# A down projection as seven block products, with weight sums made once and x in single loads

## The chip, the cores and the metric

The kernel runs on one core of a Trainium2 chip. The metric is the device time of one execution in microseconds (us). Times shown are medians over executions, and one further execution is recorded by the hardware profiler.

In the profile PE is TensorE (matmuls), PEld its weight loads, DVE is VectorE, ACT is ScalarE, POOL is GpSimd, and SP is the engine whose queue issues nearly all the transfers.

## The reference, cut to what matters

```python
x = A_x                                   # 1 x 2048 x 576
xn = layernorm(x)
q, k, v = split_heads(xn @ A_wqkv)        # 32 heads of 18
o = softmax(q @ k^T * 18**-0.5) @ v
s = merge_heads(o) @ A_wo
gate = xn @ B_W_gate                      # 576 -> 4608
up   = xn @ B_W_up
h    = relu(gate) * up                    # 2048 x 4608
g    = silu(h @ B_W_down)                 # 4608 -> 576: the down projection
return x + s * g
```

All is float32. The gated branch takes the normalized x, as the attention does.

## The kernel before, in words

**Precision.** Each float32 operand of a big product is split into a rounded high part and a low remainder ("hi" and "lo", type fp32r), and one product becomes three: hi x hi, hi x lo, lo x hi (`PRODUCTS`). ACT or POOL makes the high part with a copy, POOL or VectorE the low part with a subtraction.

**Row halves.** For the gated branch the 128 rows of TensorE are used as two halves of 64 (t = 0, 1), whose matmuls run side by side into different banks of PSUM. Where the halves change banks, a tiny ACT operation (`mark`) waits for the ends of both, and the next matmuls wait for it (`after`).

**Stages.** First come normalization, q, k and v. The parts of x for the gated branch, already split, are spilled to DRAM (`xTd`), by groups of 512 tokens (g = 0 to 3). Then 144 units follow, unit k standing for group g = k // 36 and one slice f = k % 36 of 128 hidden columns. Last comes the projection of the heads, 16 blocks of rows, with the gate applied.

**A unit** (`emit_unit`, L931). The 27 steps of `up(k)` make gate and up for 128 hidden columns and 512 tokens (9 chunks c of x, three products each). Between them an order written out by hand deals out the matmuls of the attention: from unit 16 on eight steps for scores and exponentials of one pair of heads (`exp_steps`) and eight for the row maxima of the next pair (`max_steps`, reduced by VectorE). Each row half serves one head, so a unit of 43 steps has 16 exponentials on ACT and 16 reductions. In the first 16 units there are no exponentials, and in the last eight no maxima. At the end `up_end` makes h = relu(gate) * up on ACT and VectorE, and `split_h` splits it into `hh`.

After an odd unit `attend` multiplies the exponentials with v. After an even unit `down(k - 1)` multiplies the last two units' `hh` with two slices of W_down (`rd`, split by POOL into `dw`): 4 blocks of 128 tokens x 2 halves of 288 output columns, each with 2 x 3 products and two row halves, 96 matmuls. Eight results of 128 x 288 are added to four sums `ys` (512 tokens x 576): VectorE adds six, and from unit 17 on the last two go through ACT (`add`) and POOL. Once a group is done, `gate_step` makes silu of the sums, one block of 128 tokens at a time, and stores it to `gd`.

**Queues and order.** TensorE, VectorE and POOL run in the order of the program (`mm`, `vec`, `gp` pin it). ACT's exponentials and relus, and from unit 17 on most of SP's transfers, are placed by a planner which simulates the machine; pinned ones keep their place behind what was traced before them. Buffers come from pools: five PSUM banks `psS` ("shared") rotate through scores, maxima and down products; two `psG` ("bank") hold gate and up; x has nine chunks (`xA`), read again for each group in the last unit of the group before, each as soon as its chunk is used for the last time (`load_x`, L295). `load_up` fetches the gate and up weights two units ahead; POOL splits them one unit ahead (`split_up`). Tile `e` has one buffer, shared by gates and additions.

Of the kernel before, what the change touches and what calls it, by code (L numbers as in the profile page):

```python
# [9 lines left out]
F32 = mybir.dt.float32  # L10
# [9 lines left out]
def kernel(  # L20
# [11 lines left out]
    P = 128  # L32
# [84 lines left out]
    xTd = dram.tile([NQ, XC, P, 2 * 512], F32, name="xTd")  # L117
    gd = dram.tile([S, D], F32, name="gd")
    od = dram.tile([D, S], F32, name="od")

    def bank(name):
        return psG.tile([P, 512], F32, tag="gen", name=name)
# [171 lines left out]

    def load_x(g, c):  # L295
        xc = xtile(xA)
        for t in range(2):
            pinned(
                nc.sync.dma_start(
                    xc[t * R : (t + 1) * R].rearrange("p a s -> p (a s)").bitcast(F32),  # L300
                    xTd[g, c // 2, c % 2 * R : c % 2 * R + R],
                )
            )
        xcur.setdefault(g, []).append(xc)

    with ExitStack() as st:
# [377 lines left out]
    wl = pool(mid, "wl", 2, "right")  # L684
    yp = pool(mid, "yp", 5, "right")

    def load_down(k):
        if k < len(units):
            f = units[k][1]
            if k == 1:  # L690
                rds[k] = hp.tile([P, 2, 512], F32, tag="hh", name="rd", bufs=3)
                rds[k] = rds[k].rearrange("p a s -> p (a s)")[:, :D]
            else:
                rds[k] = wl.tile([P, D], F32, name="rd", bufs=1)
            sp.dma_start(rds[k], wd[f * P : (f + 1) * P, :])

    def split_down(k):
        dws[k] = wl.tile([P, 2, D], F32R, name="dw")
        split_pool(dws[k][:, 0], dws[k][:, 1], rds.pop(k))

    def up(k):
# [27 lines left out]
    def up_end(k, ps):  # L729
        g, f = units[k]  # L730
        if f == NF - 1 and k + 1 < len(units):
            del xcur[g]
        h = hp.tile([P, 512], F32, name="h", bufs=1)
        ac.activation(h, ps[0], AF.Relu)
        vec(nc.vector.tensor_tensor(h, ps[1], h, ALU.mult))  # L735
        between.append((split_h, (k, h)))

    between = []
    hooks = {}
# [7 lines left out]

    ys = []

    def down(k):  # L750

        g, f = units[k]
        if f == 1:
            ys[:] = [yp.tile([P, D], F32, name="y") for _ in range(4)]
        terms = [(hhs.pop(k - 1), dws.pop(k - 1)), (hhs.pop(k), dws.pop(k))]
        steps = [(hh, w, a, b) for hh, w in terms for a, b in PRODUCTS]
        for q in range(2):
            parts = [(2 * q + m // 2, slice(m % 2 * HC, (m % 2 + 1) * HC)) for m in range(4)]
            outs_ = [(bank if m == 3 and q == 0 else shared)("py")[:, :HC] for m in range(4)]
            seen = []  # L760
            for turn_ in range(4):
                ends = []
                for i, (hh, w, a, b) in enumerate(steps):
                    for t in range(2):
                        rows = slice(t * R, (t + 1) * R)
                        m = ((0, 2, 1, 3), (1, 3, 0, 2))[t][turn_]
                        j, cs = parts[m]
                        ins = mm(
                            outs_[m], hh[rows, a, j * P : (j + 1) * P], w[rows, b, cs],
                            start=(turn_ < 2 and i == 0), stop=(turn_ >= 2 and i == len(steps) - 1),  # L770
                        )
                        if turn_ < 2 and i == len(steps) - 1:
                            ends.append(ins)
                        elif turn_ >= 2 and i == 0:
                            after(ins, seen[turn_ - 2])
                if turn_ < 2:
                    seen.append(pinned(nc.scalar.activation(mark, ident[:, :1], AF.Copy)))  # L777
                    for ins in ends:
                        after(seen[-1], ins)
                if q == 0 and turn_ == 1:  # L780
                    run_tasks(between)
                if q == 1 and turn_ == 3 and f > 1 and k > N1:
                    add = wl.tile([P, D], F32, tag="e", name="add", bufs=1)
                    for m in (2, 3):
                        ac.activation(add[:, parts[m][1]], outs_[m], AF.Copy)
                    gp.tensor_tensor(ys[3], add, ys[3], ALU.add)
                elif turn_ >= 2:
                    for m in range(2 * turn_ - 4, 2 * turn_ - 2):
                        j, cs = parts[m]
                        if f == 1:  # L790
                            nc.scalar.activation(ys[j][:, cs], outs_[m], AF.Copy)
                        else:
                            vec(nc.vector.tensor_tensor(ys[j][:, cs], outs_[m], ys[j][:, cs], ALU.add))  # L793
        if f == NF - 1:
            for j in range(4):
                gates.append((ys[j], g * 4 + j))
# [24 lines left out]
    def run_later():  # L821
        while later:
            later.pop(0)()
# [107 lines left out]
    def emit_unit(k, ex, ns, mx, nm):  # L931
        if k - 1 in rds:
            split_down(k - 1)
        if k not in rds and k not in dws:
            load_down(k)
        if k == 0:
            load_down(1)
        split_up(k + 1)
        if k and (units[k][1] < NF - 1 or k + 1 == len(units)):
            load_up(k + 2)  # L940
        if k == N1 + 1:
            sp.kept = False
        run_later()
        if k % 2:
            if k in rds:
                split_down(k)
            for _ in range(2):
                if to_load:
                    out_weights(to_load.pop(0))
        n = KC * len(PRODUCTS) + ns + nm  # L950
        ps, gens = up(k)
        order = []
        for t in range(2):
            due = []
            for cnt, gen, off, late in ((nm, mx, 0.0, LATE), (ns, ex, 0.25, -4)):
                due += [((i + off + t * 0.5) * (n - 1 + late) / cnt, gen[t]) for i in range(cnt)]
            due.sort(key=lambda d: d[0])
            ops = [gens[t]] * n
            free = n
            for when, gen in reversed(due):  # L960
                free = min(round(when), free - 1)
                ops[free] = gen
            order.append(ops)
        for i, (l, r) in enumerate(zip(*order)):
            next(l)
            next(r)
            if i == 8 or (i == 30 and k % 2 == 0):
                gate_step()
        if k == 0:
            split_up(2)  # L970
        up_end(k, ps)
        if k % 2 or k == 0:
            run_tasks(between)
        if k == 0:
            pinned(nc.scalar.activation(first_exp, ident[:, :1], AF.Exp))
        run_tasks(tasks)
        if k % 2:
            run_tasks(outs)
            while ready:
                attend()  # L980
        elif k:
            down(k - 1)


    wos = []

    def out_weights(c):
        rd = wl.tile([P, D], F32, name="rd", bufs=1)
# [77 lines left out]
    for u in range(NU):  # L1066
        ex = [exp_steps(u, h) for h in range(2)]
        more = u + 1 < NU
        mx = [max_steps(u + 1, h) for h in range(2)] if more else None
        if not more:  # L1070
            ac.kept = True
        for i in range(PER):
            if not more and i == 0:
                to_load[:] = range(4)
            if not more and i == PER - 1:
                fetch(0, gw_home())
                hooks[1] = [(out_weights, (4,))]
# [13 lines left out]
        split_heads(n)  # L1091
    run_tasks(outs)
    run_later()
    for n in range(16):
        if n == 2:
            down(len(units) - 1)
# [37 lines left out]
```

## Time and profile before

| | |
|---|---|
| median of 3 runs | 2584.05 us (2582.19 to 2586.38) |
| profiled execution | 2584.46 us, span 2582.7 us |
| instructions | 61529 |
| PE busy | 2569.2 us of the span |
| DVE busy | 1848.1 us |
| ACT busy | 1475.7 us |
| POOL busy | 1276.8 us |
| mean DMA rate | 99 GB/s |
| `down`, 72 times | 96 matmuls in some 6.5 us |

The page's part 5 and the answers by line give, for each group, the line, engine, operation, tile written and tiles read, then total busy time and mean of one in ns, then the idle time of the engine just ahead of it and what ended that. A line may be a helper's (L68 is every matmul, L85 every POOL operation), so groups are told apart by tiles. A timeline row gives start, duration in us (of merged instructions), engine, line, operation, tiles and count. [...]

### The profile page before, as it was taken

How to read it: one execution, taken by the hardware profiler on the slowest of the kernel's cores; microseconds unless marked ns; L12 is line 12 of the kernel's file. 1: busy time of each engine (PE TensorE's matmuls, PEld its weight loads, DVE VectorE, ACT ScalarE, POOL GpSimd, SP SyncE). 2: the span in 40 equal slices, each digit the busy share in tenths (PEclk: the TensorE clock that was granted, in tenths of full speed). 3: DMA queues.
4: the chain of work that ended last, by engine and by line, in shares of the span. 5: the costliest groups of instructions: out<-in, count | busy, mean ns of one | idle time of the engine just before them, and what ended most of it. 6: DMA issues, size and time to landing. Idle time of an engine off the chain costs nothing.

```text
span 2582.7 us, 61529 instructions
## 1 busy us (share of the span) xinstructions
PE 2569.2 (99%) x25301; PEld 2022.1 (78%) x25301; DVE 1848.1 (72%) x3019; ACT 1475.7 (57%) x3005; POOL 1276.8 (49%) x1003
## 2 busy tenths in 40 slices
PE   9999999999999999999999999999999999999999
PEld 8899987777677777877767777777777777777779
DVE  6336677777777778877777777887777777778127
ACT  3222146666666666666666666666656666666662
POOL 5246764444464444444455444444436444444555
PEclk9999999999999999999999999999999999999999
DMA  8866432323543223223263323332354233222237
GB/s 250 282 206 150 103 85 49 86 65 81 125 109 73 70 71 73 65 68 74 72 160 79 76 68 72 72 75 59 80 122 115 69 74 72 69 63 59 68 103 232
DMA packets 263833, 254.60 MB, mean 99 GB/s; under 512 B 27648, under 2 KB 208640, under 8 KB 263552
## 3 DMA queue, kind: packets, MB, share of 16 engines
q1 hardware_dynamic: 255808, 223.01, 35.1%
q0 software_dynamic: 7744, 27.66, 3.1%
q8 instruction: 199, 3.26, 0.5%
q14 instruction: 82, 0.67, 0.1%
HBM read 203.54 MB, written 46.53 MB: 97 GB/s over the span
## 4 chain that ended last, share of the span: by engine, by line
PE 95%; DMA 3%; POOL 1%; DVE 1%; ACT 0%; issue 0%; SPq 0%; POOLq 0%; ACTq 0%
PE pg L68 32%; PE py L68 18%; PE po L68 17%; PE pm L68 10%; PE psx L68 9%; PE pq L68 4%; PE pw L68 2%; DMA x<-xTd 2%; PE pv L68 2%; PE tps L76 0%; DMA rd<-in_A_wo_dram 0%; POOL gw L85 0%; DMA xt<-in_A_x_dram 0%; POOL y L85 0%; POOL kq L85 0%
## 5 line engine op out<-in xcount | busy, mean ns | idle before, releaser
L268 DVE TENSOR_REDUCE mx<-pm 128x1 f32<-128x512 f32 x2048 | 1371.6, 690 | 368.8 <-PE pm L68 261.9
L68 PE MATMUL pg<-x,gw 64*128 64x512 f32 x7533 | 1359.4, 392 | 6.0 <-DMA x<-xTd 6.0
L97 ACT ACTIVATE p<-psx 128x512 f32<-128x512 f32 x2048 | 1098.3, 604 | 208.6 <-PE psx L68 167.3
L68 PEld LDWEIGHTS pg<-x,gw 64*128 64x128 f32 x7533 | 1019.7, 186 | 106.4 <-DMA x<-xTd 10.2
L85 POOL TENSOR_TENSOR hh<-h,hh 128x512 fp32r<-128x512 f32 x144 | 185.7, 1289 | 808.2 <-ACT hh L743 804.5
L68 PE MATMUL py<-dw,hh 64*128 64x288 f32 x6912 | 478.2, 292 | 0.1
L68 PEld LDWEIGHTS py<-dw,hh 64*128 64x128 f32 x6912 | 473.3, 185 | 6.1 <-ACT h L97 0.7
L68 PE MATMUL po<-p,va 128*32 128x512 f32 x4096 | 452.7, 594 | 0.0
L85 POOL TENSOR_TENSOR gw<-rg,gw 128x1152 fp32r<-128x1152 f32 x131 | 350.2, 2673 | 10.5
L68 PEld LDWEIGHTS po<-p,va 128*32 128x32 f32 x4096 | 126.5, 110 | 291.5 <-issue 280.2
L793 DVE TENSOR_TENSOR y<-py,y 128x288 f32<-128x288 f32 x422 | 171.9, 453 | 140.0 <-PE py L68 140.0
L68 PE MATMUL psx<-qT,kq 56*128 56x512 f32 x608 | 230.8, 393 | 0.0
L68 PE MATMUL pm<-kq,qT 54*128 54x512 f32 x608 | 225.6, 395 | 0.3 <-ACT p L97 0.3
L85 POOL TENSOR_TENSOR dw<-rd,dw 128x576 fp32r<-128x576 f32 x144 | 206.5, 1434 | 11.5
L68 PE MATMUL psx<-kq,kA 56*128 56x512 f32 x512 | 195.2, 394 | 0.0
L68 PE MATMUL psx<-kq 56*128 56x512 f32 x512 | 194.8, 393 | 0.0
L68 PE MATMUL pm<-kA,kq 54*128 54x512 f32 x512 | 192.4, 398 | 0.5 <-ACT p L97 0.4
L68 PE MATMUL pm<-kq 54*128 54x512 f32 x512 | 191.1, 397 | 0.0
L85 POOL CAST gw<-rg 128x1152 fp32r<-128x1152 f32 x131 | 154.6, 1180 | 73.7 <-PE py L68 36.3
L777 ACT ACTIVATE mark<-ident 128x1 f32<-128x1 f32 x288 | 58.4, 203 | 219.1 <-PE py L68 219.0
L85 POOL TENSOR_TENSOR y<-add,y 128x576 f32<-128x576 f32 x61 | 87.4, 1433 | 180.0 <-ACT add L97 180.0
L743 ACT ACTIVATE hh<-h 128x512 fp32r<-128x512 f32 x144 | 90.8, 631 | 123.4 <-DVE h L735 123.4
(99 smaller groups left out, 2542.6 us busy)
## 6 DMA issues: line engine op xcount, KB each, us to landing
rd<-in_B_W_down_dram SPq DMA_DIRECT2D x144, 288.0 KB
rg<-in_B_W_gate_dram SPq DMA_DIRECT2D x131, 288.0 KB
rg<-in_B_W_up_dram SPq DMA_DIRECT2D x131, 288.0 KB
x<-xTd SPq DMA_DIRECT2D x72, 256.0 KB
qd<-hh POOLq DMA_DIRECT2D x16, 512.0 KB, 4.1
kd<-hh POOLq DMA_DIRECT2D x16, 512.0 KB, 5.6
xTd<-x SPq DMA_DIRECT2D x16, 512.0 KB
kq<-kd SPq DMA_DIRECT2D x210, 36.0 KB
```

Of the source, the lines that this page charges most:

```text
L68: return tc.keep_in_program_order(nc.tensor.matmul(*args, **kw))
L85: return lambda *args, **kw: tc.keep_in_program_order(op(*args, **kw))
L97: i = op(*args, **kw)
L268: vec(nc.vector.tensor_reduce(mx[:, h, b, j, c : c + 1], ps, axis=AX.X, op=ALU.max))
L743: copy = nc.scalar.activation(hhs[k][:, 0], h, AF.Copy)
L777: seen.append(pinned(nc.scalar.activation(mark, ident[:, :1], AF.Copy)))
L793: vec(nc.vector.tensor_tensor(ys[j][:, cs], outs_[m], ys[j][:, cs], ALU.add))
```

## The change

In groups 1 to 3 (54 of the 72 pairs of units) `down_made` takes the place of `down`. A pair's two slices of hidden columns, two halves of 256 tokens and two halves of 288 output columns make a 2 x 2 block product; by Strassen's identity seven products replace eight. Each product has 2 blocks of 128 tokens, three precision products and two row halves, opened in one visit of six matmuls and closed in a second, so a pair has 84 matmuls. The seven products are kept in seven sums a half group (`a`, `b`, `c`, `d`), added by ACT with POOL (seven of 14) and VectorE (seven); `combine` puts them together on POOL at the end of a group.

The left operands need sums and differences of blocks of h (`first_half`, `second_half`: POOL sums and lows, ACT high parts, emitted at steps 2, 8 and 13 of the following unit). The right ones need sums of blocks of W_down: `make_items` makes and splits all 18 x 7 of them during group 0, three in a unit up to unit 15 and five after that, and stores them to DRAM (`wtd`, 295 KB each); `load_w` reads seven a pair. The sums of weights are added on VectorE up to unit 15 and on POOL after it.

Also changed: a chunk of x is read by one transfer whose source is 64 rows taken twice, instead of two transfers; group 0's last `load_down` moves behind the steps of unit 35; `gate_step` moves from steps 8 and 30 to 17 and 27; `ys` has four buffers, not five; h has two.

```diff
     def load_x(g, c):
         xc = xtile(xA)
-        for t in range(2):
-            pinned(
-                nc.sync.dma_start(
-                    xc[t * R : (t + 1) * R].rearrange("p a s -> p (a s)").bitcast(F32),
-                    xTd[g, c // 2, c % 2 * R : c % 2 * R + R],
-                )
+        pinned(
+            nc.sync.dma_start(
+                xc.rearrange("p a s -> p (a s)").bitcast(F32),
+                xTd[g, c // 2, c % 2 * R : c % 2 * R + R].unsqueeze(0).to_broadcast([2, R, 1024]),
             )
+        )
...
+    MS = (0, 3, 4, 6, 2, 1, 5)
...
+    def first_half(h):
+        def raws():
+            nc.scalar.activation(a[:, 0, s], h[:, s], AF.Copy)
+            gp.tensor_tensor(r[:, s], h[:, z], h[:, s], ALU.subtract)
+            nc.scalar.activation(a[:, 0, z], r[:, s], AF.Copy)
+        def lows():
+            low(a, s, h[:, s])
+            low(a, z, r[:, s])
...
+        return {2: [raws], 8: [lows]}
...
+    def second_half(hs):
+        def raws():
+            nc.scalar.activation(b[:, 0, z], h2[:, z], AF.Copy)
+            gp.tensor_tensor(r[:, s], h2[:, s], h2[:, z], ALU.subtract)
+            nc.scalar.activation(b[:, 0, s], r[:, s], AF.Copy)
+            gp.tensor_tensor(r[:, z], h1[:, s], h2[:, z], ALU.add)
+            nc.scalar.activation(d[:, 0], r[:, z], AF.Copy)
+        def lows():
+            low(b, z, h2[:, z])
+            low(b, s, r[:, s])
+            low(d, s, r[:, z])
...
+            gp.tensor_tensor(r[:, :512], h1, h2, ALU.add)
+            nc.scalar.activation(c[:, 0], r[:, :512], AF.Copy)
+        def rest():
+            low(c, slice(0, 512), r[:, :512])
...
+        return {2: [raws], 8: [lows], 13: [rest]}
...
+    def down_made(k):
+        def visit(p, swap):
+            for i, (a, b) in enumerate(PRODUCTS):
+                for t in range(2):
+                    j = t ^ swap
+                    ins = mm(
+                        outs_[p][j], h[rows, a, (o + j) * P : (o + j + 1) * P], w[rows, MS[p], b],
...
+        def by_scalar(p, j):
+            src = add_home()
+            pinned(nc.scalar.activation(src, outs_[p][j], AF.Copy))
+            gp.tensor_tensor(dst, src, dst, ALU.add)
...
+        def opened(p):
+            outs_[p] = [(bank if j and p in (1, 4) else shared)("py")[:, :HC] for j in range(2)]
+            ends = visit(p, 0)
+            seen[p] = pinned(nc.scalar.activation(mark, ident[:, :1], AF.Copy))
...
+        def closed(p):
+            visit(p, 1)
+            by = (by_scalar, by_scalar) if p == 0 else (by_vector, by_vector) if p == 6 else (by_scalar, by_vector)
...
+        opened(0)
+        for p in range(7):
+            if p + 1 < 7:
+                opened(p + 1)
+            closed(p)
...
+        if f == NF - 1:
+            todo = [(combine, (j,)) for j in range(2)]
+                at_step[11] = [lambda: run_tasks(todo[:1])]
+                at_step[21] = [lambda: run_tasks(todo[1:])]
...
+    def make_items(fp):
+        def start(m, on):
+                    gp.tensor_tensor(t, x0, x1, op)
+            s_ = pw.tile([P, 2, HC], F32R, name="ws")
+            nc.scalar.activation(s_[:, 0], x0, AF.Copy)
+        def end(m):
+            gp.tensor_tensor(s_[:, 1], x0, s_[:, 0].bitcast(F32), ALU.subtract)
+            sp.dma_start(wtd[fp, m], s_.bitcast(F32))
...
-            if i == 8 or (i == 30 and k % 2 == 0):
+            if i in (17, 27):
                 gate_step()
+            if k < NF and k:
+                per = 3 if k < N1 else 5
+                if any(i == 2 + q * (n - 3) // per for q in range(per)):
+                    make_step(nc.vector if k < N1 else nc.gpsimd)
+            if k > NF:
+                pr = (k - 1) // 2
+                late = units[2 * pr + 1][1] == NF - 1 and 2 * pr + 2 < len(units)
+                if late == (k % 2 == 0) and i >= 1 and i % 4 == 1 and i // 4 < 7:
+                    load_w(pr % (NF // 2), [MS[i // 4]])
```

More of the change, by code (lines that the diff above doesn't have):

```diff
@@ L119 @@
     od = dram.tile([D, S], F32, name="od")
+    wtd = dram.tile([NF // 2, 7, P, 2, HC], F32, name="wtd")
     def bank(name):
@@ L683 @@
     pp = pool(mid, "pp", 8, "right")
-    wl = pool(mid, "wl", 2, "right")
-    yp = pool(mid, "yp", 5, "right")
+    wl = pool(mid, "wl", 1, "right")
+    yp = pool(mid, "yp", 4, "right")
+    plain = mid.enter_context(ExitStack())
+    pw = pool(plain, "pw", 2, "right")
+    made = mid.enter_context(ExitStack())
+    mw = []
     def load_down(k):
-        if k < len(units):
+        if k < NF:
             f = units[k][1]
@@ new lines, with load_w, sums_of @@
+    made_w = {}
+    def load_w(fp, ms):
+        if not made_w:
+            made_w["w"] = mw[0].tile([P, 7, 2, HC], F32R, name="w", bufs=1)
+        for m in ms:
+            sp.dma_start(made_w["w"][:, m].bitcast(F32), wtd[fp, m])
+    acc = {}
+    def sums_of(m, j):
+        a = acc["a", j], acc["b", j], acc["c", j]
+        return {
+            0: a[2][:, :HC], 1: a[1][:, :HC], 2: a[0][:, HC:], 3: a[2][:, HC:],
+            4: acc["d", 0][:, j * HC : (j + 1) * HC], 5: a[1][:, HC:], 6: a[0][:, :HC],
+        }[m]
@@ new lines, in combine @@
+    def combine(j):
+        a, b, c = acc["a", j], acc["b", j], acc["c", j]
+        l, r = slice(0, HC), slice(HC, D)
+        m5 = acc["d", 0][:, j * HC : (j + 1) * HC]
+        for d, s_, op in (
+            (a[:, l], c[:, l], ALU.add), (a[:, l], c[:, r], ALU.add), (a[:, l], m5, ALU.subtract),
+            (b[:, r], c[:, l], ALU.add), (b[:, r], b[:, l], ALU.subtract), (b[:, r], a[:, r], ALU.add),
+            (a[:, r], m5, ALU.add), (b[:, l], c[:, r], ALU.add),
+        ):
+            gp.tensor_tensor(d, d, s_, op)
@@ new lines, with load @@
+    items = []
+    def make_items(fp):
+        st = {}
+        def load():
+            st["w"] = pw.tile([P, 2, D], F32, name="wp", bufs=1)
+            for i in range(2):
+                f = 2 * fp + i
+                sp.dma_start(st["w"][:, i], wd[f * P : (f + 1) * P, :])
+        def start(m, on):
+            w = st["w"]
+            b = [[w[:, i, c * HC : (c + 1) * HC] for c in range(2)] for i in range(2)]
+            x0, x1, op = {
+                0: (b[0][0], b[1][1], ALU.add), 1: (b[0][0], None, None), 2: (b[0][1], b[1][1], ALU.subtract),
+                3: (b[1][0], b[0][0], ALU.subtract), 4: (b[1][1], None, None), 5: (b[0][0], b[0][1], ALU.add),
+                6: (b[1][0], b[1][1], ALU.add),
+            }[m]
+            if op is not None:
+                t = pw.tile([P, HC], F32, name="wt")
+                if on is nc.vector:
+                    vec(on.tensor_tensor(t, x0, x1, op))
+                else:
+                    gp.tensor_tensor(t, x0, x1, op)
+                x0 = t
+            s_ = pw.tile([P, 2, HC], F32R, name="ws")
+            nc.scalar.activation(s_[:, 0], x0, AF.Copy)
+            st[m] = x0, s_
+        def end(m):
+            x0, s_ = st.pop(m)
+            gp.tensor_tensor(s_[:, 1], x0, s_[:, 0].bitcast(F32), ALU.subtract)
+            sp.dma_start(wtd[fp, m], s_.bitcast(F32))
+        return [(load, start, end, m) for m in (None, 1, 4, 0, 2, 3, 5, 6)]
@@ L750, in down, with make_step @@
+    for fp in range(NF // 2):
+        items.extend(make_items(fp))
+    open_items = []
+    def make_step(on):
+        while open_items:
+            end, m = open_items.pop()
+            end(m)
+        if items:
+            load, start, end, m = items.pop(0)
+            if m is None:
+                load()
+            else:
+                start(m, on)
+                open_items.append((end, m))
     def down(k):
+        if k >= NF:
+            down_made(k)
+            return
         g, f = units[k]
@@ L933, in emit_unit @@
             split_down(k - 1)
-        if k not in rds and k not in dws:
+        steps = dict(at_step)
+        at_step.clear()
+        if k not in rds and k not in dws and k != NF - 1:
             load_down(k)
@@ L966, in emit_unit @@
             next(r)
-            if i == 8 or (i == 30 and k % 2 == 0):
+            for fn in steps.get(i, ()):
+                fn()
+            if i in (17, 27):
                 gate_step()
+            if k < NF and k:
[7 more added lines that the diff above has]
+                    load_w(pr % (NF // 2), [MS[i // 4]])
         if k == 0:
             split_up(2)
+        if k == NF - 1:
+            load_down(k)
         up_end(k, ps)
@@ L982, in emit_unit @@
             down(k - 1)
+            if k == NF:
+                while items or open_items:
+                    make_step(nc.gpsimd)
+                plain.close()
+                mw.append(pool(made, "mw", 1, "right"))
     wos = []
     def out_weights(c):
-        rd = wl.tile([P, D], F32, name="rd", bufs=1)
+        rd = wl.tile([P, D], F32, tag="e", name="rd", bufs=1)
         if c < 4:
@@ L1076 @@
                 fetch(0, gw_home())
-                hooks[1] = [(out_weights, (4,))]
+                hooks[5] = [(out_weights, (4,))]
                 hooks[2] = [(split_heads, (0,))]
@@ L1093 @@
     run_later()
+    for _, fns in sorted(at_step.items()):
+        for fn in fns:
+            fn()
     for n in range(16):
```

87 lines of the change are left out of this document (83 added, 4 removed).

## The prediction, on record before the run

> **What bounds the kernel now.** I read the page first: busy times and the chain that ended last.
>
> ```profile
> span 2582.7 us, 61529 instructions
> PE 2569.2 (99%) x25301; PEld 2022.1 (78%) x25301; DVE 1848.1 (72%) x3019; ACT 1475.7 (57%) x3005; POOL 1276.8 (49%) x1003
> PE 95%; DMA 3%; POOL 1%; DVE 1%; ACT 0%; issue 0%; SPq 0%; POOLq 0%; ACTq 0%
> ```
>
> TensorE is busy for 99% and carries 95% of the chain, so matmuls that go shorten the run, as long as what feeds TensorE keeps up. Then the groups of instructions by line; the durations below are the means of these rows.
>
> ```profile
> L68 PE MATMUL py<-dw,hh 64*128 64x288 f32 x6912 | 478.2, 292 | 0.1
> L793 DVE TENSOR_TENSOR y<-py,y 128x288 f32<-128x288 f32 x422 | 171.9, 453 | 140.0 <-PE py L68 140.0
> L97 ACT ACTIVATE add<-py 128x288 f32<-128x288 f32 x122 | 43.5, 409 | 80.0 <-PE py L68 80.0
> L777 ACT ACTIVATE mark<-ident 128x1 f32<-128x1 f32 x288 | 58.4, 203 | 219.1 <-PE py L68 219.0
> L85 POOL TENSOR_TENSOR gw<-rg,gw 128x1152 fp32r<-128x1152 f32 x131 | 350.2, 2673 | 10.5
> L85 POOL CAST gw<-rg 128x1152 fp32r<-128x1152 f32 x131 | 154.6, 1180 | 73.7 <-PE py L68 36.3 <-DMA rg<-in_B_W_up_dram 30.8 <-PE po L68 3.9
> L85 POOL TENSOR_TENSOR hh<-h,hh 128x512 fp32r<-128x512 f32 x144 | 185.7, 1289 | 808.2 <-ACT hh L743 804.5 <-DMA rg<-in_B_W_up_dram 2.5 <-DMA kq<-kd 1.1
> L85 POOL TENSOR_TENSOR y<-add,y 128x576 f32<-128x576 f32 x61 | 87.4, 1433 | 180.0 <-ACT add L97 180.0
> L85 POOL TENSOR_SCALAR e<-e 128x576 f32<-128x576 f32 x16 | 11.0, 686 | 0.1
> ```
>
> Last the windows and the timeline of one ordinary pair of units in group 2: 9.9 us of steps, 6.5 us of `down`, 10 us of steps, 7.1 us of `attend`.
>
> ```profile
> 1511.30:1521.20 9.90, 9.90 (x88) 8.50 (x86) 8.88 (x14) 9.23 (x17) 1.39 (x3) 1.00 0.32 68
> 1521.20:1527.70 6.50, 6.50 (x98) 6.46 (x96) 4.54 (x10) 2.04 (x6) 1.29 (x1) 1.00 0.12 27
> 1527.70:1537.70 10.00, 10.00 (x92) 8.85 (x88) 9.29 (x16) 9.22 (x18) 8.64 (x7) 1.00 0.12 31
> 1537.70:1544.80 7.10, 7.10 (x68) 1.98 (x64) 5.39 (x8) 1.23 (x2) 3.92 (x4) 1.00 0.72 167
> sum 33.50, PE 33.50 PEld 25.79 DVE 28.10 ACT 21.72 POOL 15.24; mean PE 8.38 PEld 6.45 DVE 7.03 ACT 5.43 POOL 3.81
> 1512.08 9.02 ACT L97 ACTIVATE p<-psx 128x512 f32<-128x512 f32 x16
> 1521.20 1.89 DVE L268 TENSOR_REDUCE mx<-pm 128x1 f32<-128x512 f32 x3
> ```
>
> Columns of a window: length, then busy time (and count) of PE, PEld, DVE, ACT, POOL, clock, DMA share, GB/s. TensorE never pauses in the pair, at full clock. ACT's sixteen exponentials fill the steps, and VectorE is still reducing 1.9 us into `down`.
>
> **The products.** `down` issues 96 matmuls a pair, `down_made` 7 x 2 x 6 = 84. A matmul costs 478.2 us / 6912 = 69 ns, two row halves running together. Twelve fewer in 54 pairs: 54 x 12 x 69 ns = **-44.8 us**. That is all the change can take from the matmuls.
>
> **Banks and evacuations in the product.** Evacuations of 288 columns rise from 8 to 14 a pair (7 on ACT, 7 on VectorE): 7 x 409 + 7 x 203 ns of marks = 4.3 us on ACT in a 5.8 us product, so ACT has room; what matters is when. A visit of six matmuls takes 0.41 us. The third product opens after three visits, 1.2 us in, and needs the fourth and fifth shared bank; VectorE's last reduction (to 1523.1) frees the fifth only 1.7 us or so after `down` began: 0.4 us of waiting, where the old order needed that bank 3.3 us in. The first mark comes after one visit instead of two (0.1 us), and the fourth product needs both banks that ACT alone evacuates. ACT's copies further on wait for a home in `e`, which is free when POOL has added (about 0.8 us each, below). I take 0.65 us a pair, **+35 us**; bounds 0.1 and 1.0 us (no waiting but the first mark; each of these waits in full), +5 to +54. So the products alone are nearly a draw.
>
> **Splitting the hidden sums.** The new 256-column operations cost POOL about 0.7 us and 288 columns 0.8 us (from 1289 ns at 512 and 1433 ns at 576, 2.2 ns a column). POOL loses the splits of `dw`, gains 8 such pieces, two of 512 and seven adds, and stays near 22 us of a 33.5 us pair: hidden. ACT gets copies of 256 and one of 512 columns among exponentials that fill 9.0 of 9.9 us; half a microsecond of lateness is bridged by the five banks. I take 0.15 us a pair, **+8 us** (0 to +25).
>
> **Weight sums in group 0.** 126 products are made in units 1 to 35, with 37 MB stored by SP. From unit 16 a pair holds ten items, some nine with a product: 9 x 0.8 us of subtractions and 6 x 0.8 us of adds on POOL, on top of its 15.2 us, 27 us; between add and subtraction it waits for ACT's copy (some 0.6 us, 6 times), 31 us of 33.5. POOL is then almost the bound, ACT queues behind it, and each copy needs a `ws` buffer whose store has landed. 1.5 us in ten pairs: **+15 us** (0 to +40). SP's stores stand ahead of loads that are issued a unit before use: no cost while that unit covers them.
>
> **x in single loads.** This carries the forecast. Now the boundary of a group:
>
> ```profile
> 1291.81 0.36 SPq L97 DMA_DIRECT2D rd<-in_B_W_down_dram  x1
> 1292.27 16.12 SPq L299 DMA_DIRECT2D x<-xTd  x18
> 1309.10 0.65 SPq L97 DMA_DIRECT2D rg<-in_B_W_gate_dram  x1
> 1294.00:1308.00 14.00, 14.00 (x126) 7.53 (x124) 8.59 (x15) 7.37 (x15) 4.97 (x4) 1.00 1.03 237
> 1304.40:1317.80 13.40, 11.33 (x93) 8.47 (x91) 9.11 (x14) 9.73 (x18) 0.00 (x0) 1.00 1.08 225
> 1317.56 1.72 PE L68 MATMUL py<-dw,hh 64*128 64x288 f32 x21
> ```
>
> Eighteen loads of 256 KB saturate all 16 DMA engines at 237 GB/s; the unit takes 13.4 us of which 2.1 are idle, and its `down` starts at 1317.6. The new load halves SP's issues, and no `rd` load stands ahead of it. But its source is a pattern of 2 x 64 rows, the outer 2 with no stride. How many engines does a load get? Compare one load of `nr` (outermost dimension 2) with one `rd` load (128 rows), each alone in its window:
>
> ```profile
> DMA  0000000000000111110000000000000000000000
> DMA packets 18, 0.00 MB, mean 3 GB/s; under 512 B 18, under 2 KB 18, under 8 KB 18
> DMA  0018999359016393898959698661302010000000
> DMA packets 144, 0.29 MB, mean 147 GB/s; under 512 B 16, under 2 KB 16, under 8 KB 144
> q1 hardware_dynamic: 144, 0.29, 51.9%
> ```
>
> `rd` has 128 rows and 16 small packets more, and its slices reach 9 tenths of the engines; `nr` has 16 runs and 2 small packets more, and never passes 1 tenth, as 2 of 16 engines would (0.125). So I read: a load is spread by its outermost dimension, and a source whose outermost dimension is 2 runs on two engines. Each then moves 256 KB a load. Speed of a busy engine: 237 GB/s / (16 x 1.03) = 14.4 GB/s at saturation, 0.29 MB / (0.519 x 16 x 2 us) = 17.5 for `rd`, and from the row of the other queue,
>
> ```profile
> q0 software_dynamic: 7744, 27.66, 3.1%
> ```
>
> 27.66 MB / (0.031 x 16 x 2582.7 us) = 21.6. With two engines alone I take the fastest: 262144 B / 21.6 = 12.1 us a load, 109 us for nine (18.2 and 164 us at saturation; 80 us if a lone engine is a third faster than any row). From 1288.5, when the first buffer is free, the last x lands near 1399 and `down` could start at 1400 instead of 1317.6: **+82 us**, at the three boundaries **+247 us** (160 to 410).
>
> [...]
>
> **Behind the loads.** `rg` shares those two engines and lands after x; POOL's in-order queue has `split_up(73)` (1.2 + 2.7 us) ahead of `second_half`, so the hidden sums come some 9 to 11 us after x, at two boundaries. In the next unit `combine` puts 16 x 0.8 us and the four gates 4 x (0.7 + 1.4) us on POOL, beside two `gw` splits of 3.9 and some 9 of hidden sums: 38 us for a 33.5 us pair, before POOL's own waits for the gates' Tanh: the following `down_made` waits about 10 us and its `b` sums, still being stored by the gate, 3 more. Together 2 x 24 = **+48 us** (10 to 60). At the start the seven x loads issued by 116 us, and the last two at 196 us, are late too:
>
> ```profile
> 82.01 33.72 SPq L299 DMA_DIRECT2D x<-xTd  x14
> 195.88 4.10 SPq L299 DMA_DIRECT2D x<-xTd  x3
> L68 PE MATMUL pg<-x,gw x7533: 383/392/502, 199.3 to 2505.1; 64*128 64x512 f32 x199
> ```
>
> Two loads at 12.1 us from 196 end near 222, where unit 0 would want the last x some 7 us after its start at 199: **+20 us** (0 to 45). The weight loads (2 MB a pair) run a unit ahead: 0.
>
> Sum: -45 + 35 + 8 + 15 + 247 + 48 + 20 = +328 on the profiled execution's 2584.46 us (span 2582.7; the median, 2584.05, is the same within 0.02%): **2912 us**. With all bounds low 2715, high 3174; they will not all go one way: 2760 to 3080.
>
> **Rivals.** (1) *All sixteen engines.* If the load is spread by the 128 rows of its destination, x costs no more than now, and 2 to 3 us a boundary go because no `rd` load delays SP: -8. If POOL's chains are hidden as well (their low ends), the sum is -45 + 20 (downs) + 4 + 5 - 8 = -24: **2560 us, faster**. It decides at SP's loads in units 35, 71 and 107: under some 26 us for nine loads they hide in their two units. For it: the destination does have 128 rows, and the old loads with 64 ran at 237 GB/s. Against it: `nr`, whose source has 16 partitions, still ran on two. (2) *All sixteen engines, but POOL and ACT eat the gain:* -45 + 35 + 8 + 15 + 48 - 8 = +53 - some slack: **2630 us**. For it: VectorE's 1.9 us tail and POOL's 38 us. (3) *Draw:* the waits in the product equal its twelve matmuls and the loads are hidden: **2585 us**.
>
> **Chances.** The two-engine load 0.68; rival 1 0.17; rival 2 0.11; rival 3 0.04. Within 0.2% (5 us) is what a measurement here can't tell from no change. Faster 0.17, same 0.04, slower 0.79. To leave out no more than 2 in 10 the range goes from 2570 to 3060; the likeliest case's own is 2760 to 3080.
>
> **What would show it.** Right: small packets fall by 36 x 30 for x (two a load instead of 2 x 16); in units 36, 72 and 108 DMA share near 0.13 for 80 to 160 us, with TensorE idle and released by x<-xTd; matmuls py down by 648; POOL busy near nine tenths in units 16 to 35; a TensorE wait for hidden sums after each x. Wrong: x at the old bandwidth, or steps at boundaries of 10 to 14 us; then the forecast is too high by some 300 us. If `down_made` lasts under 5.9 us, my bank waits are not there.

## The result

| | before | after |
|---|---|---|
| median | 2583.12 us (2582.09 to 2586.38, 4 runs) | 3605.05 us (3602.46 to 3614.0, 4 runs) |
| ratio | | 1.3959, 95% interval 1.3932 to 1.3987 |
| profiled execution, span | 2584.46, 2582.7 us | 3614.0, 3612.2 us |
| mean granted clock of TensorE | 1.000 | 0.876 |

Slower, as forecast, but by 1022 us and not by 328. The page of the kernel after: span, the row of busy times, the granted clock in 40 slices (tenths of full speed), and the chain that ended last.

```profile
span 3612.2 us, 63126 instructions
PE 2920.0 (81%) x24653; PEld 2138.8 (59%) x24653; DVE 1898.3 (53%) x3118; ACT 1710.9 (47%) x3761; POOL 1737.2 (48%) x1762
PEclk9978888888868989998976999899985999999899
PE 31%; POOL 31%; DMA 9%; ACT 5%; issue 4%; SPq 1%; DVE 0%; ACTq 0%; POOLq 0%; DVEq 0%
```

TensorE has 648 matmuls fewer and is busy for 351 us more, since its clock fell from 1.000 to 0.876. The chain, 95% TensorE before, now runs as much over POOL, though POOL is busy for only 48%. The waits of TensorE, ACT and POOL (engine and tile, what released it; us in total, times, longest):

```profile
PE psx L68 <- ACT p L97: 422.5, 135, 42.4
PE pg L68 <- DMA x<-xTd: 72.7, 12, 10.1
ACT ha L779 <- POOL hr L85: 233.8, 54, 13.3
ACT hb L802 <- POOL hr L85: 211.0, 54, 45.7
ACT ws L965 <- DMA wtd<-ws: 168.6, 42, 19.0
ACT hc L817 <- POOL hr L85: 163.2, 54, 3.0
POOL gw L85 <- PE pg L68: 436.7, 46, 10.4
```

TensorE waits for a bank that ACT's exponentials (`p`) have not emptied; ACT waits for POOL's sums of the hidden values (`hr`, 54 times each, once a pair) and for the weight sums (`ws`); POOL in its turn waits for TensorE to free the weights' buffer (`gw`). In an ordinary pair of group 2, timeline and windows (here and below, rows in between are left out):

```profile
2631.72 3.09 POOL L85 TENSOR_TENSOR c<-add,c 128x288 f32<-128x288 f32 x4 [11.79 <-ACT add L879]
2634.76 2.33 POOL L85 TENSOR_TENSOR y<-add,y 128x288 f32<-128x288 f32 x3
2637.04 1.14 POOL L85 CAST gw<-rg 128x1152 fp32r<-128x1152 f32 x1
2638.26 2.63 POOL L85 TENSOR_TENSOR gw<-rg,gw 128x1152 fp32r<-128x1152 f32 x1
2640.84 0.73 POOL L85 TENSOR_TENSOR hr<-h 128x256 f32<-128x256 f32 x1
...
2641.60 0.42 ACT L779 ACTIVATE ha<-hr 128x256 fp32r<-128x256 f32 x1 [4.23 <-POOL hr L85]
2641.92 2.06 ACT L97 ACTIVATE p<-psx 128x512 f32<-128x512 f32 x4
...
2642.55 0.79 PE L68 MATMUL psx<-qT,kA 56*128 56x512 f32 x1 [3.46 <-ACT p L97]
2643.64 0.63 PE L68 MATMUL psx<-qT,kA 56*128 56x512 f32 x1
2648.68 0.39 PE L68 MATMUL psx<-qT,kA 56*128 56x512 f32 x1
```

```profile
2636.30:2653.10 16.80, 13.34 (x90) 9.90 (x92) 9.94 (x16) 9.35 (x18) 6.74 (x8) 0.80 0.56 159
1150.00:1825.00 675.00, 605.41 (x5103) 423.75 (x5105) 431.89 (x702) 400.13 (x870) 334.58 (x345) 0.91 0.33 93
```

ACT's copy of `hr` is in its queue ahead of the exponentials. POOL reaches `hr` only after its seven additions of the product before (5.4 us) and the split of the next weights (3.8 us), so ACT stands 4.23 us, TensorE 3.46 us, and behind the pause a matmul takes some 0.62 instead of 0.39 us for over 5 us. The steps of this unit last 16.8 us; POOL was busy for 6.7 of them. A pair (from one product's start to the next) takes 42.4 us in group 1, where before took 33.7. Over 1150 to 1825, 15.9 such pairs, TensorE stood 69.6 us, 4.4 a pair: half of the 8.7 lost. Most of the rest is the clock of 0.91: 0.09 x 675 us are 61 us, 3.8 a pair, less what fell into the pauses themselves.

The following runs take the changed kernel apart. For e1 to e4 the time is that of one execution (before: 2584.16 us beside them), for the others a median, with the ratio to before and its interval.

### The profile page after: what moved, and what is told of

It is laid out like the page before. It is cut to its first block, busy times and chain, and to the rows that moved or that the text cites. A ratio compares the mean times of both kernels' runs of the same rounds, so it can differ in the third digit from the quotient of the medians.

```text
span 3612.2 us, 63126 instructions
## 1 busy us (share of the span) xinstructions
PE 2920.0 (81%) x24653; PEld 2138.8 (59%) x24653; DVE 1898.3 (53%) x3118; ACT 1710.9 (47%) x3761; POOL 1737.2 (48%) x1762
## 4 chain that ended last, share of the span: by engine, by line
PE 31%; POOL 31%; DMA 9%; ACT 5%; issue 4%; SPq 1%; DVE 0%; ACTq 0%; POOLq 0%; DVEq 0%
PE pg L68 15%; POOL gw L85 12%; PE psx L68 6%; PE pm L68 5%; POOL hr L85 5%; POOL y L85 4%; POOL c L85 4%; DMA x<-xTd 3%; PE py L68 3%; ACT p L97 2%; DMA rg<-in_B_W_up_dram 2%; POOL hb L85 2%; PE pw L68 1%; SPq L97 1%; DMA wtd<-ws 1%
## 5 line engine op out<-in xcount | busy, mean ns | idle before, releaser
L68 PE MATMUL pg<-x,gw 64*128 64x512 f32 x7533 | 1624.8, 439 | 86.4 <-DMA x<-xTd 72.7
L68 PEld LDWEIGHTS pg<-x,gw 64*128 64x128 f32 x7533 | 1135.5, 212 | 238.3 <-DMA x<-xTd 79.3
L85 POOL TENSOR_TENSOR c<-add,c 128x288 f32<-128x288 f32 x204 | 157.9, 807 | 584.3 <-ACT add L879 584.3
L68 PE MATMUL psx<-qT,kA 56*128 56x512 f32 x416 | 185.8, 461 | 119.3 <-ACT p L97 119.3
L68 PE MATMUL pm<-kA,kq 54*128 54x512 f32 x512 | 220.2, 455 | 28.8 <-DMA kA<-kd 19.0
L68 PEld LDWEIGHTS psx<-qT,kq 56*128 56x128 f32 x608 | 128.4, 211 | 161.4 <-ACT p L97 146.2
L68 PE MATMUL pm<-kA,qT 54*128 54x512 f32 x416 | 172.1, 436 | 23.9 <-ACT p L97 23.9
L739 DVE TENSOR_TENSOR h<-pg,h 128x512 f32<-128x512 f32 x144 | 98.3, 683 | 159.5 <-ACT h L97 107.6
L965 ACT ACTIVATE ws<-wt 128x288 fp32r<-128x288 f32 x90 | 39.8, 443 | 298.6 <-DMA wtd<-ws 158.5
L68 PEld LDWEIGHTS psx<-kq 56*128 56x128 f32 x512 | 110.9, 217 | 114.7 <-ACT p L97 101.8
L68 PEld LDWEIGHTS psx<-kq,kA 56*128 56x128 f32 x512 | 109.0, 213 | 116.8 <-ACT p L97 104.1
```

Of the source, the lines that this page charges most:

```text
L68: return tc.keep_in_program_order(nc.tensor.matmul(*args, **kw))
L85: return lambda *args, **kw: tc.keep_in_program_order(op(*args, **kw))
L965: nc.scalar.activation(s_[:, 0], x0, AF.Copy)
```

## Experiments: where the 1022 us lie

**e1, x in two loads again.** The changed kernel with the old `load_x`.

```diff
-            nc.sync.dma_start(xc..., xTd[g, c // 2, ...].unsqueeze(0).to_broadcast([2, R, 1024]))
+        for t in range(2):
+            nc.sync.dma_start(xc[t * R : (t + 1) * R]..., xTd[g, c // 2, ...])
```

> The changed kernel with x loaded as before, in two transfers of 64 rows a chunk. Theory A (the single load runs on two of 16 engines, and this is one of three separate losses): the units at the three group boundaries fall from 82 to some 13 to 16 us and the start loses its 30 us, so about 240 us come off 3605: 3340 to 3400 us. Rival (x only hides other waits, which then show): under 100 us come off.

3367.39 us: the single load costs 238 us here.

**e2, the kernel before with the single load of x alone.** The opposite edit on the other kernel.

> The kernel before with nothing changed but the single load of x. Theory A: nine loads of some 10 us on two engines, +60 to 75 us at each of three boundaries and +20 to 35 us at the start: 2790 to 2850 us. Rival (in the changed kernel the loads were slow because the weight loads queued with them): within 30 us of 2583.

2865.14 us, +281. In its trace the boundary pairs take 113.0 us instead of 36.3 to 37.0 (76 each; forecast 82). The start costs 50 us, where 20 were forecast and 45 was the bound: unit 0 starts at 228.8 instead of 199.3 us, and its first product at 270.3 instead of 220.2. SP's queue and TensorE's waits from 190 to 300 us:

```profile
81.66 74.88 SPq L298 DMA_DIRECT2D x<-xTd  x7
PE pm L68 <- DMA kA<-kd: 19.0, 1, 19.0
PE po L68 <- DMA x<-xTd: 17.1, 2, 10.3
```

The first seven loads hold SP's queue for 74.9 us instead of 33.7, so loads of the attention behind them (`kA`) come late too, and inside unit 0 TensorE waits for the last two chunks of x. These waits are 36 of the 50 us. Page and window of e2, busy share of the DMA engines in 40 slices of 1432 to 1502 us:

```profile
DMA packets 262752, 254.59 MB, mean 89 GB/s; under 512 B 26568, under 2 KB 207560, under 8 KB 262472
DMA  1111111111111111161111111111111111111111
GB/s 51 56 51 51 51 48 41 51 54 51 54 51 51 51 51 51 68 166 44 51 54 51 54 51 35 49 54 51 51 51 54 51 51 51 51 51 51 54 51 51
```

Small packets (under 512 B) fall from 27648 to 26568, by 1080 = 36 x 30, two a load instead of 32; the share is one tenth and the rate 51 GB/s, some 25.5 for each of two engines. A load takes some 10.2 us (I had 12.1 from 21.6 GB/s).

**e8, the same single loads from 128 plain rows.** This kernel reads another chunk's rows in half of the places.

```diff
-            xTd[g, c // 2, c % 2 * R : c % 2 * R + R].unsqueeze(0).to_broadcast([2, R, 1024])
+            xTd[g, min(c // 2, 3)]
```

> The kernel before with x in single loads whose source is 128 plain rows in place of 2 x 64 with no stride between (half of the rows read are another chunk's, so the values are not x's; bytes, destination and number of loads are those of the change). Theory (the outermost dimension of the source sets the engines: 2 gave 2): 16 engines, no loss at the change of group, 2575 to 2588 us, 52 to 53 x-free packets fewer a group and DMA share near 1 there. Rival (any single load of this size is slow, or the destination or SP's order is at fault): 2800 us or more, as with the pattern of 2 x 64.

2576.71 us, ratio 0.9975 (0.9966 to 0.9984): 7 us under before, about what rival 1 gave x on sixteen engines (-8). The window 1288 to 1308 us:

```profile
DMA  0079999579648988998899999999999999999999
q1 hardware_dynamic: 2654, 5.64, 92.1%
```

Same bytes, same destination, as many loads, and all engines work: the pattern of the source was the cause. Its 2 in the outermost dimension came with a stride of zero, and no run here takes only one of them away; the prediction's `nr` loads, with a 2 and no such stride, never passed 1 tenth either, which speaks for the 2.

**e3, the hidden sums ahead of the splits.** e1 with POOL's split of the next weights moved behind the first sums, and ACT's copies of the results some steps later, so that they find them ready.

```diff
-        return {2: [raws], 8: [lows]}
+        return {2: [raws], 9: [high], 10: [lows]}     # high: ACT's copy of hr
...
-        split_up(k + 1)
+        steps.setdefault(10 if k % 2 else 14, []).append(next_up)     # split_up and load_up
```

> x in two loads, and from unit 37 on POOL does the hidden sums before the split of the next gate and up weights (which moves from the start of a unit to step 10 or 14), with ACT's copies of the late sums placed where the sums are ready. No work is added or taken away. Theory B (ACT, in order, stood waiting for POOL's sums behind that split, and TensorE behind ACT): an ordinary pair of units in groups 1 to 3 falls from some 42.5 us to 34 to 36, some 300 to 450 us less than with x alone: 2920 to 3080 us. Rival C (ACT's additional copies themselves, or the 2 MB of weight loads a pair, slow the steps): less than 80 us under x alone.

2999.64 us: with the same instructions 368 us are gone. Ordinary pairs take 34.4 us. Over 12.7 of them TensorE is busy without a break at full clock:

```profile
1150.00:1586.00 436.00, 435.95 (x4033) 315.10 (x4031) 333.86 (x557) 313.68 (x685) 270.62 (x274) 1.00 0.40 111
```

**e4 and e5, one pair's weight sums alone.** e1 (e4) and e3 (e5) with the sums of the first pair of slices only, read by all pairs; 17 of 18 pairs are left out.

```diff
-    for fp in range(NF // 2):
-        items.extend(make_items(fp))
+    items.extend(make_items(0))
```

> x in two loads, and the weight sums of the first pair alone are made; every pair reads these seven. It leaves out 17 of 18 pairs of weight sums with their loads, copies and stores. Theory D (the sums in group 0 cost some 290 us by holding ACT): units 0 to 35 fall to some 10 us over those of before, 250 to 300 us under x alone: 3070 to 3130 us. Rival (what holds group 0 is the slow start after x): under 80 us.

> Three repairs at once: x in two loads, POOL making the hidden sums ahead of the next weights' split, and only the first pair's weight sums (17 of 18 pairs of slices are left out, so the numbers it multiplies with are not the reference's). If the three losses are independent, as my theory says, the rest adds: e3's 2999.6 minus the 261.5 us that e4 took off e1 = 2738 us (2715 to 2765), and what is left over before (154 us) lies in the pair after each change of group (some 30 us each, combine and the gates on POOL), in the last pairs and in some 0.7 us an ordinary pair. Rival: the losses overlap (one slow engine hidden behind another), then 2650 us or less, or over 2800 us.

e4 took 3105.90 us, 261 less than e1; e5 2736.46 us (ratio 1.0595, 1.0578 to 1.0613), 263 less than e3. So the losses add: 238 for x, 368 for the order of the hidden sums, some 262 for the weight sums, and 153 that stay in e5. Of these, by the pairs in its trace: the pair after a change of group 67.4 and 66.1 us instead of 35.0 and 34.3 (64 in two); the two pairs in which the last maxima are done and W_o is loaded 41.7 and 41.4 instead of 30.2 (23); the start of group 1 14; units 0 to 16 17; the rest mostly 0.8 us in each ordinary pair.

## Experiments: the weight sums in group 0

ACT's waits for `ws` in units 0 to 35 of e3:

```profile
ACT ws L968 <- DMA wtd<-ws: 136.2, 39, 13.8
ACT ws L968 <- POOL wt L85: 110.4, 42, 7.8
ACT ws L968 <- DMA wp<-in_B_W_down_dram: 77.2, 28, 13.6
```

Three releasers, so three repairs were tried, in this order.

**e6, later and with more buffers.** e3 with ACT's copy one step after its sum, three buffers of `ws` for two, the raw pair loaded a step earlier.

```diff
+        def high(m):                       # one step after start(m), one before end(m)
+            s_ = pw.tile([P, 2, HC], F32R, name="ws", bufs=3)
+            pinned(nc.scalar.activation(s_[:, 0], st[m], AF.Copy))
```

> e3 with all weight sums made, but each high part (ACT) made one step after its sum, the subtraction one step later still, three buffers for ws instead of two, and the next pair of raw slices loaded a step earlier. Same work, other order. Theory (ACT in its order waits for a store, a load or POOL, and the exponentials stand behind it): group 0 loses much of its 261 us, 2800 to 2890 us, ACT's waits for ws fall from some 340 us to under 150. Rival (the amount of work on POOL is what costs): 2960 us or more, POOL busy over nine tenths in units 17 to 34.

2919.52 us (ratio 1.1308, 1.1291 to 1.1325): 80 of 262 back, less than the theory's 110 to 200.

**e9, stores from POOL.** e6 with `gp.dma_start(wtd[fp, m], ...)` in place of `sp.dma_start`.

> e6 with one more edit: the stores of the weight sums are issued by POOL, right behind the subtraction that they store, and no longer by SP. Theory (SP works in its order: a load of rd waits up to 16 us there for POOL's split of dw, the stores stand behind it, ACT's copies wait for their buffers and the exponentials for ACT): of the 187 us that e6 still loses in units 0 to 34 some 100 to 150 go, 2770 to 2830 us, and ACT's waits for the stores of ws fall from 98 to under 25 us. Rival (the stores themselves are slow, or the work of ACT and POOL is too much): 2880 us or more.

2930.18 us (1.1341, 1.1323 to 1.1358): nothing gained, though each store now takes POOL 0.56 us. ACT's waits for the stores stay at 100.3 us (e6: 97.8; forecast under 25), so my theory of SP's queue falls. The timeline shows what ACT stands behind:

```profile
565.05 1.44 POOL L85 TENSOR_TENSOR y<-add,y 128x576 f32<-128x576 f32 x1 [3.32 <-ACT add L97]
567.18 1.43 POOL L85 TENSOR_TENSOR dw<-rd,dw 128x576 fp32r<-128x576 f32 x1
569.78 2.63 POOL L85 TENSOR_TENSOR gw<-rg,gw 128x1152 fp32r<-128x1152 f32 x1
573.10 1.40 POOL L85 TENSOR_TENSOR dw<-rd,dw 128x576 fp32r<-128x576 f32 x1
574.45 0.79 POOL L85 TENSOR_TENSOR ws<-wt,ws 128x288 fp32r<-128x288 f32 x1
...
579.37 0.44 ACT L971 ACTIVATE ws<-wp 128x288 fp32r<-128x288 f32 x1 [9.84 <-POOL ws L85]
```

POOL's first subtraction of the unit comes after a block of three splits; the buffers behind it are not free until then, and ACT stands 9.84 us.

**e13, the splits spread.** e6 with the splits at steps 8 and 24 of odd and 6 and 22 of even units.

> e6 with POOL's splits of W_down and of the next gate and up weights no longer in one block of some 10 us at the start of the units 17 to 34, but apart, at steps 8 and 24 of an odd unit and 6 and 22 of an even one; the same operations and stores. Theory (in e9's unit 25 POOL does the sum of y and three splits from 565 to 574 us, ACT waits 9.8 us behind them for a buffer of ws and TensorE 9.6 us for ACT: the order of POOL's queue is what costs, as with the hidden sums): of the 187 us that e6 loses in units 0 to 34 the 115 us of units 17 to 34 fall to under 40, 2800 to 2855 us in all. Rival (too much work for POOL and ACT in these units, or slow stores): 2900 us or more.

2886.76 us (1.1170, 1.1155 to 1.1185): 33 more back, between theory and rival.

**e15 and e16, ACT kept out.** e3 and e13 with POOL making the high part too.

```diff
-            nc.scalar.activation(s_[:, 0], x0, AF.Copy)
+            gp.tensor_copy(s_[:, 0], x0)
```

> e3 with one edit: the high part of each weight sum is copied by POOL and no longer by ACT, so that ACT, the engine of the exponentials, has nothing to do with the weight sums and cannot wait for them. POOL gets 126 copies of 288 columns more (an estimate of 0.45 us each from the 0.68 us of 576 columns, 57 us). Theory (what costs is that ACT, in order, stands behind POOL, a store or a load, wherever these come from): of the 261 us in group 0 under 90 are left, 2780 to 2830 us, and TensorE's waits for the exponentials there nearly vanish. Rival (group 0 has too much work for POOL, or its transfers are too slow, whoever makes the copies): 2930 us or more.

> The same edit on e13 (splits spread, three buffers of ws, wp a step earlier). Theory: ACT free of the sums, POOL's block of splits gone: 2745 to 2800 us, within 60 us of e5, which makes one pair of sums alone. Rival (the amount of work): POOL with some 31 us of work in 33.7 us falls behind, 2850 us or more.

e15 took 2851.70 us (1.1038, 1.1019 to 1.1056), 148 less than e3 by this one edit, though 22 above the forecast's upper end; e16 2799.99 us (1.0836, 1.0820 to 1.0852), at the upper end of the forecast and 64 above e5 (forecast: within 60). Units 17 to 34, e3 and then e16 (before took 303.4 us for them):

```profile
470.00:945.00 475.00, 359.71 (x2967) 256.52 (x2966) 239.25 (x384) 216.72 (x461) 247.32 (x244) 0.86 0.37 111
```

```profile
437.40:750.20 312.80, 307.27 (x2993) 233.27 (x2992) 236.15 (x387) 191.85 (x380) 276.24 (x324) 0.99 0.55 169
```

POOL has more work in e16, is busy for 88% instead of 52%, and the stage takes 313 instead of 477 us. So the amount of work was not what cost; ACT's place in line behind it was. In e15, whose splits stay in one block, TensorE waits for POOL's `gw` instead (28.0 us). Most of what is left in e16 lies in units 0 to 16 (238.8 us, e5 184.3) and was not taken apart further.

## Experiments: the clock after a pause

**e7, ACT late in small pieces.** The kernel before with 14 copies of 128 columns on ACT in each odd unit from 17 on.

> The kernel before with one thing added: 14 small copies on ACT (some 3.5 us, results unchanged) in one place of every odd unit from 17 on, 64 times, so that the exponentials come late and TensorE pauses 2 to 3 us. Theory (a pause costs itself and then some, since TensorE's granted clock is low for about 6 us after it: in the changed kernel the matmuls behind a 3.5 us pause went at 0.43 instead of 0.23 us a piece): 64 x (2.3 + 2.6) = +314 us, 2840 to 2950 us, granted clock under 0.95 overall. Rival (the clock fell for another reason, such as the extra work of the other engines): at most 64 x 3.5 = +224 us, less what five banks bridge, some 2730 us, clock 1.00.

2805.33 us (1.0864, 1.0848 to 1.0880), clock 0.996. This did not make the pause it was meant to: the copies fell among the exponentials, no wait of TensorE ahead of unit 136 was over 0.64 us, and 64 units lost 3.5 us each, about the work added to ACT. Waits that short left the clock alone here: it was 1.00 over 950 to 1020 us, where TensorE stood 3.4 of 70 us.

**e10, the pause in one piece.** In each even unit from 18 on, ACT copies 128 columns, POOL does 14 small operations on them, ACT waits for the last: the chain of the hidden sums by itself.

> The kernel before with a pause in one piece, made as the hidden sums made it: at step 3 of 63 even units ACT copies 128 columns, POOL does 14 small operations one after another on them (some 5 us), and ACT waits for the last; results unchanged. TensorE should stand still for some 4 us at a time, where e7's pauses were of 0.6 us or less and the clock stayed at 0.996. Theory (a pause of over a microsecond or so is followed by 4 to 6 us at about half the pace): 63 x (4 + 2.3) = +400 us, 2900 to 3050 us, granted clock 0.92 to 0.96, matmuls at 0.62 us behind each pause. Rival (a pause costs its own length, as in e7): 63 x 4 = +250 us, 2780 to 2850 us, clock 0.99 or more.

3080.08 us (1.1920, 1.1903 to 1.1936), clock 0.926. Timeline and window of one pair:

```profile
972.85 6.12 POOL L85 TENSOR_TENSOR dm<-dm 128x128 f32<-128x128 f32 x13
979.00 0.20 ACT L976 ACTIVATE dn<-dm 128x1 f32<-128x1 f32 x1 [5.22 <-POOL dm L85]
979.74 0.79 PE L68 MATMUL pm<-kq 54*128 54x512 f32 x1 [4.54 <-ACT p L97]
984.17 0.62 PE L68 MATMUL pm<-kA,kq 54*128 54x512 f32 x1
985.00 0.39 PE L68 MATMUL psx<-qT,kq 56*128 56x512 f32 x1
946.90:987.90 41.00, 36.46 (x338) 26.99 (x336) 28.31 (x46) 21.55 (x45) 21.39 (x25) 0.92 0.24 59
```

The pause is 4.54 us, the slow stretch behind it 5.3 us, and the pair takes 41.0 instead of 33.7 us: 7.3, of which 2.8 are the clock. The total passes the forecast by 30 us: a pair lost 7.3 us where 6.3 were forecast, and at the three changes of group and in two of the last pairs POOL came later still (pauses of 13.6 to 13.9, 14.9 and 16.1 us). In the slow stretch TensorE went at about half its pace (0.43 instead of 0.23 us from one step to the next). Shorter pauses did it too: in the changed kernel 1.43 us were enough in most cases (last section).

## Experiments: what the kernel before loses at x

**e11, x stored in 128 rows.** Every half chunk stored twice, 18 stores a group instead of 5, one plain load a chunk.

> The kernel before with x stored in the rows in which it is loaded (each half twice, 18 stores a group of tokens instead of 5), so that each chunk comes in one load of 128 plain rows; results unchanged. By the theory of e8 the change of group costs nothing any more; the stores add 4.7 MB in the first 200 us. If those are hidden: 2574 to 2580 us; if the start is as much longer as its writes take at 237 GB/s: +20 us, 2595 us.

2598.42 us (1.0060, 1.0047 to 1.0073). The later stages are those of e8, but unit 0 starts at 227.0 instead of 199.3 us: the stores are not hidden.

**e12, the `rd` load behind the steps; e14, the same load at step 22.**

```diff
-        if k not in rds and k not in dws:
+        if k not in rds and k not in dws and not last_rd:
             load_down(k)
...
+            if i == 22 and last_rd:        # e12: i == n - 1
+                load_down(k)
```

> The kernel before with one load moved: in the last unit of each group the raw slice of W_down is loaded behind the unit's steps and no longer ahead of the x loads in SP's order; x in two loads as before. In the kernel before the first x load is issued only when that slice's buffer is free, and the unit takes 13.4 us instead of 10 at three boundaries. Theory (SP's order delays x): 2575 to 2581 us, 0.1 to 0.35% faster. Rival (the loads themselves take that long at 237 GB/s): 2584 us.

> The kernel before with the raw slice of W_down of each group's last unit loaded at step 22, among the x loads, and not ahead of them (before) nor behind all steps (e12, where the boundary unit was 2.8 to 3.4 us shorter, but the pair after it 2.5 to 5.4 us longer, since its split of dw came late). Theory: both ends are kept, 2574 to 2580 us, 0.15 to 0.4% faster than before. Rival (SP's place in line is not what sets the unit; the x loads need their 13 us at 237 GB/s): 2583 us or more.

e12 took 2589.64 us (1.0020, 1.0011 to 1.0028): the boundary pairs fell from 36.3, 36.7 and 37.0 to 33.7, but the next ones rose from 35.0, 35.0 and 34.3 to 37.4, 40.4 and 39.4. The gain was given back as a wait for the late split:

```profile
PE py L68 <- POOL dw L85: 9.9, 6, 2.5
```

e14 keeps both ends: 2576.64 us (0.9971, 0.9959 to 0.9983). Of the versions that leave nothing out it is the one that is faster than both kernels, by 0.3% against before. SP now issues x from 1286.7, not 1292.3:

```profile
1286.69 6.23 SPq L299 DMA_DIRECT2D x<-xTd  x10
1293.02 0.54 SPq L97 DMA_DIRECT2D rd<-in_B_W_down_dram  x1
1293.67 7.97 SPq L299 DMA_DIRECT2D x<-xTd  x8
```

## Why the prediction was right in its sign and wrong in its size

| step of the prediction | forecast | measured |
|---|---|---|
| products and their bank waits | -10 | +13 to +20 (0.24 to 0.37 us a pair) |
| splitting the hidden sums | +8 | +368, and some 0.4 us a pair that stay in e3 |
| weight sums in group 0 | +15 | +262, some 84 of it in units 0 to 16 |
| x in single loads, three boundaries | +247 | +229 (e2) |
| x in single loads, the start | +20 | +50 (e2) |
| both together | +267 | +281 alone, +238 in the changed kernel |
| behind the loads | +48 | +64 (e5, with x in two loads) |
| not foreseen: the last pairs, units 0 to 16, start of group 1 | 0 | +54 in e5 |

**x** was right in mechanism: two engines, shown by e2 (a DMA share of one tenth) and e8 (nine tenths). Each ran at some 25.5 GB/s, above my fastest row (21.6), and within the "third faster" of the low bound. That the sum came so close was partly luck, since the boundaries cost 18 us less than forecast and the start 30 more, past its bound of 45. The start counted only the two loads at its end. The seven early ones held SP's queue for 41 us longer, and loads that TensorE needed before unit 0 stood behind them.

**The products** are nearly a draw, as forecast. With the matmul at 68 ns (6.58 us / 96), 84 need 5.76 us; from the first start to the last end they took 6.82 in the changed kernel and 6.96 in e3. So the waits are 1.1 to 1.2 us a pair and not 0.65, just past the upper bound of 1.0. The bank wait named is there (timeline of e3):

```profile
1241.12 1.89 DVE L269 TENSOR_REDUCE mx<-pm 128x1 f32<-128x512 f32 x3
1242.80 0.92 PE L68 MATMUL py<-w,hc 64*128 64x288 f32 x6
1244.24 0.68 PE L68 MATMUL py<-w,hc 64*128 64x288 f32 x6
```

The third product opens at 1242.80, but goes on only when VectorE's last reduction ends (1243.01); the visit takes 0.92 us, one that waits for nothing 0.68. By the starts of the matmuls three other visits are held up for 0.2 us or more, which I had not counted.

**"Splitting the hidden sums"** is the step that failed first. It compared POOL's work with the pair (22 of 33.5 us) and called it hidden. But POOL and ACT took this work in the order of their queues: the sum stood behind 9.2 us of other work on POOL, ACT's copy waited for it, and fifteen of the sixteen exponentials waited for the copy. The "half a microsecond of lateness" was 4.2 us, and 3.0 us for `hc`. e3 shows it: the same work in another order takes 368 us less.

**"Weight sums in group 0"** failed in the same way. POOL was to be "almost the bound", near nine tenths; it was at 52%, because it waited too. "1.5 us in ten pairs" were some 19 us in each of the nine pairs of units 17 to 34 (53 a pair on average in e3 instead of 33.7), and e16, with POOL at 88%, lost least: the load that was forecast was not what cost. Units 0 to 16, which the term left out, took 269.0 us in e3 and 184.3 in e5.

**"Behind the loads"** came near in size, but not by the waits that it named, and its part for the late x is not in e5 at all. In e5's pair of 67.4 us TensorE stood 16.4 us for exponentials, while ACT stood 18.0 us for POOL's sums `y` ahead of the gates, and 7.6 us for the load of `w`; the weight loads had been put at 0.

**The clock** was in no term. A pause of TensorE cost about half as much again in e10 (2.8 us for 4.54), and nearly twice itself in the changed kernel (8.7 us a pair, 0.8 of it there without pauses too, for 4.4 us of pauses).

Of the rivals none came: they all had x on 16 engines. Rival 2's mechanism (POOL and ACT eat the gain) was right, but as 153 + 368 + 262 us, not as 53.

## What to carry to other kernels

When work is added to an engine that looks idle, do not compare its busy time with the span: list what stands ahead of it in that queue, who waits in order for its result, and what is queued behind the one who waits. If an engine that feeds the bottleneck has to wait for a slower one, place its copy after the result is ready, or give the copy to the slower engine. And look at the outermost dimension of a transfer: with 2 there, at a stride of zero, loads of 512 KB ran on two engines here, at 51 GB/s.

## What the runs showed of the hardware that I had not expected

- A pause of 4.5 us cost TensorE some 2.8 us more in clock (e10); waits of up to 0.64 us cost none (e7, where it was 1.00 over 950 to 1020 us). In the changed kernel a pause of 1.43 us also lowered the clock, about a microsecond after work had begun again, for some 3.7 us. By the granted clock (0.79 over the 8 us behind each) so did 19 of the 22 pauses of 1.42 to 1.46 us in its ordinary pairs; the other three are the first of each group, and the window behind one of them (ended at 1177.05) has a clock of 1.00. What decides between them is not known.

```profile
1517.44 0.49 PE L68 MATMUL psx<-qT,kq 56*128 56x512 f32 x1 [1.43 <-ACT p L97]
1519.59 0.63 PE L68 MATMUL psx<-qT,kq 56*128 56x512 f32 x1
1523.10 0.39 PE L68 MATMUL psx<-qT,kq 56*128 56x512 f32 x1
1177.10:1189.10 12.00, 12.00 (x117) 10.13 (x119) 9.99 (x16) 10.20 (x23) 1.74 (x3) 1.00 0.19 57
```

- Two DMA engines alone moved some 25.5 GB/s each (51 GB/s together in e2), where each of sixteen moved 14.4 in the prediction's saturated window.
